# A gate's down-projection made transposed and turned by copies, with six output row buffers

## The chip, the cores and the metric

The kernel runs on one core of one Trainium2 chip. Its engines are TensorE (PE, with its weight loads shown as PEld), VectorE (DVE), ScalarE (ACT), GpSimd (POOL) and SyncE (SP), which issues nearly all copies. The metric is the device time of one execution in microseconds (us), the median of several runs.

## The reference

One attention layer and one gated feed-forward layer read the same normalised rows (2048 tokens, 640 features, all bf16). The feed-forward result, through a silu, gates the attention's result:

```python
xn = _layernorm(x, axis=-1)                       # x: 1 x 2048 x 640
# attention: 32 heads of 20, softmax over all 2048 keys
qkv = (xn @ wqkv).reshape(B, S, 3, 32, 20)
s = concat_heads(softmax(q @ k.T * 20**-0.5) @ v) @ wo
# gated feed-forward, 640 -> 1728 -> 640
h = sigmoid(xn @ w_gate) * (xn @ w_up)
g = silu(h @ w_down)
return x + s * g
```

(`concat_heads` stands for the transpose and reshape that put the 32 heads side by side again.)

## The kernel before

A first stage, about the first 30 us, loads the rows, normalises them and keeps them transposed in `xnT` (128 features on the partitions, 5 blocks of features, 4 chunks of 512 tokens). After it the kernel is one long stage whose instruction order on PE, ACT, DVE and POOL is written out by a planner: a loop over a modelled time `now` that picks, for each engine that is free in its model, the next piece of work. The chip then runs this order as it stands, engine by engine, with waits between the engines.

What the planner orders:

* Attention, in 32 blocks of 4 heads and 512 queries. PE makes score tiles (128 keys x 512 queries, line 900) into PSUM: two double banks `scA` that ACT reads with one exponential over 1024 columns (`pt`), and three single banks `bk`. A score tile in a single bank is either read by ACT (`px`, 512 columns) or by DVE, which makes the exponential itself in integer arithmetic (`iv`, then three passes over four tiles, `pb`). PE multiplies all of them with the values into `oacc` (line 937). At the end of a block `norm_a` and `norm_b` copy `oacc` (`on`), turn the sums of the exponentials by copies through DRAM (`ld`, `lt`), take a reciprocal on DVE (`rt`), spread it by copies (`rd`, `rl`), multiply on POOL (`on_bf`) and copy the result into `oU`.
* The feed-forward layer, `glu_items`, chunk by chunk: 14 gate and up projections (`mk_gu`) fill `hT` (hidden features on the partitions, 512 tokens), then the down-projection (`mk_down`). These items take one of the three single banks that the scores use too.
* The output projection (`mk_out`), two halves of 320 features for each of the first 12 token tiles: PE multiplies `oU` with `wo`, DVE multiplies the result with the gate row (`otmp`), POOL or DVE adds the row of x, and SP writes the result. The last chunk's four token tiles are made by a chain of their own at the very end (`chain`).

In the down-projection of before, an item is one token tile of 128 and one half of 320 features. `cols` puts each of its 14 steps on PE as four matmuls side by side that each use 32 columns of the array; the tokens' hidden values are the stationary operand and `wd` streams, 320 columns. ACT takes a tanh of the result (`td`), and DVE combines both (`gqs`, line 741; in the last chunk `gql`, line 737) to four times the silu. The result has tokens on the partitions, as the output needs it, in f32. For chunks 0 to 2 SP writes it to `gq_dram`; `load_out` later reads a token tile's row of it beside the row of x, into one of three buffers cut from `xnT`, for the token tile at hand and the one after it within a chunk. For the last chunk it stays in SBUF (`gq_last`).

What sets the order around the change: `LEAD` (how far, in us of PE work, the feed-forward items may run ahead of a due line), `M_ORD`, `DORD` and `XORD` (which of the three single banks an item, a DVE score tile or an extra ACT score tile takes first), the events `ev_at` that an item's `pre` waits for, and the list `timed`, whose entries are put into the SP queue when the model's time comes. SP issues its copies strictly in order, and a copy that waits holds those behind it. `timed` is one way for copies to get there; the others are issued with the instruction that makes their data.

Of the kernel before, what the change touches and what calls it, by code (L numbers as in the profile page):

```python
# [29 lines left out]

URGENT, ROUNDS, HOLD, SLACK, LEAD, LAG, D_LAST, D_LAST_END = 0.2, 6, 0.0, 0.0, 40.0, 2.0, 20, 20
M_ORD, WAIT3, FALL, M_END = 1, 0.2, 1, 2.0
NPT, NPX, NPB, NIV = 12, 5, 3, 3
DVE_ADD = 8
XMAX, DQ, DORD, XORD, STARVE = 2, 1.4, 2, 0, 0.3

# [16 lines left out]
def kernel(  # L53
# [40 lines left out]

    gq_dram = dram.tile([S, D], FP32, name="gq_dram", tag="gqd", bufs=1)
    NU = (HEADS - PG * GH) // UH
# [350 lines left out]
    T_IV, T_ON = 0.605, 0.60  # L447
    LATE, T_LT, T_OU, T_L2, T_RL = 1.0, 9.0, 1.5, 4.5, 5.6
    T_PASS = (0.1333, 0.1333, 0.27)
# [215 lines left out]
    def mk_gu(c, kf, at):  # L665
# [20 lines left out]
        def th():  # L686
            st["t"] = w2.tile([P, QC], BF16, tag="tnh", bufs=2, name="tnh")
            act_imm(st["t"][0:fs, :], st["g"][0:fs, :], ACT.Tanh, 0.5)
# [8 lines left out]
        def th2():  # L697
            st["t"] = w2.tile([P, QC], BF16, tag="tnh", bufs=2, name="tnh")
            act_imm(st["t"][fs:P, :], st["g"][0:fs, :], ACT.Tanh, 0.5)
# [13 lines left out]

    def gq_last(t4):
        if len(gq_l) == t4 // 2:
            w = w2.tile([P, 2, KD, 2 * P], BF16, tag="wgu", bufs=2, name="gql")
            gq_l.append(w.rearrange("p i k f -> p (i k f)").bitcast(FP32))
        return gq_l[t4 // 2][:, t4 % 2 * D:(t4 % 2 + 1) * D]

    def mk_down(c, t4, h, at):  # L720
        st = {}
        tt = 4 * c + t4

        def alloc():
            st["ps"] = misc_ps()

        def mm(kf):
            cols(st["ps"][:, 0:HD], hT[:, kf, t4 * P:(t4 + 1) * P], wd[:, kf, h * HD:(h + 1) * HD],
                 kf == 0, kf == NFT - 1)

        def th():
            st["td"] = w2.tile([P, HD], BF16, tag="td", bufs=2, name="td")
            act_imm(st["td"], st["ps"][:, 0:HD], ACT.Tanh, 0.25)

        def ev():
            if c == NQC - 1:
                return nc.vector.scalar_tensor_tensor(out=gq_last(t4)[:, h * HD:(h + 1) * HD], in0=st["td"], scalar=1.0,
                                                      in1=st["ps"][:, 0:HD], op0=ALU.add, op1=ALU.mult)
            flush("o")
            gqs = w2.tile([P, HD], FP32, tag="gqs", bufs=3, name="gqs")  # L740
            ins = nc.vector.scalar_tensor_tensor(out=gqs, in0=st["td"], scalar=1.0, in1=st["ps"][:, 0:HD],
                                                 op0=ALU.add, op1=ALU.mult)
# [13 lines left out]
    def div_scale(tps, n):  # L756
# [6 lines left out]
        return onq  # L763

    def load_out(tt):
# [4 lines left out]
        out_tiles[tt] = (o2[:, 0:D], o2[:, D:3 * D].bitcast(FP32))  # L770
        nc.sync.dma_start(out=out_tiles[tt][0], in_=x2[tt * P:(tt + 1) * P, :])
        nc.sync.dma_start(out=out_tiles[tt][1], in_=gq_dram[tt * P:(tt + 1) * P, :])

    def mk_out(tt, h, at):
        st = {}

        def alloc():
            if h == 0:
                load_out(tt)
                if (tt + 1) % 4:  # L780
                    load_out(tt + 1)
            st["ps"] = misc_ps()
# [5 lines left out]
        def ev():  # L788
            xr, gqr = out_tiles[tt]
            sl = slice(h * HD, (h + 1) * HD)  # L790
            while sum(x[1] == "o" for x in pool_q) > 2:
                x = next(x for x in pool_q if x[1] == "o")
                pool_q.remove(x)
                x[2]()
            tmp = w2.tile([P, 2 * HD], BF16, tag="gqs", bufs=3, name="otmp")[:, 0:HD]
            ins = nc.vector.scalar_tensor_tensor(out=tmp, in0=st["ps"][:, 0:HD], scalar=0.25,
                                                 in1=gqr[:, sl], op0=ALU.mult, op1=ALU.mult)

            if tt >= DVE_ADD:
                st["tmp"] = tmp  # L800
                return ins

            def part(i):
                cs = slice(h * HD + i * HD // 2, h * HD + (i + 1) * HD // 2)
                add = nc.gpsimd.tensor_tensor(out=xr[:, cs], in0=tmp[:, i * HD // 2:(i + 1) * HD // 2], in1=xr[:, cs], op=ALU.add)
                if h == 1 and i == 1:
                    nc.sync.dma_start(out=out2[tt * P:(tt + 1) * P, :], in_=xr)
                return add
            for i in range(2):
                pool_q.append((now + 0.6, "o", lambda i=i: part(i)))  # L810
            return ins
        def add():
            xr = out_tiles[tt][0][:, h * HD:(h + 1) * HD]
            ins = nc.vector.tensor_tensor(out=xr, in0=st["tmp"], in1=xr, op=ALU.add)
            if h == 1:
# [3 lines left out]
                     ("DVE", 0.40, ev, "free", mark("o", tt, h))] + ([("DVE", 0.24, add)] if tt >= DVE_ADD else []), at, need=ALT + 1 + 2 * (tt // 4),  # L819
                    pre=[("d", tt // 4, t4, i) for t4 in range(4) for i in range(2)] + [("h", 2, kf) for kf in range(NFT)] + (  # L820
                        [("o", tt - 2, 1)] if h == 0 and tt > 1 else []))
# [284 lines left out]
    def t_main(t4):  # L1106
        nc.vector.scalar_tensor_tensor(out=tmps[t4], in0=mains[t4], scalar=0.25, in1=gq_last(t4)[:, 0:512],
                                       op0=ALU.mult, op1=ALU.mult)
        if t4 < 2:
            nc.gpsimd.tensor_tensor(out=tail[t4][:, 0:512], in0=tmps[t4], in1=tail[t4][:, 0:512], op=ALU.add)  # L1110

    def t_rest(i):
        nc.vector.scalar_tensor_tensor(out=tmp[:, 2 * i:2 * i + 2, :],
                                       in0=rest[i][:, 0:2 * EX].rearrange("p (t e) -> p t e", e=EX),
                                       scalar=0.25, in1=gq_l[i].rearrange("p (t u) -> p t u", u=D)[:, :, 512:D],
                                       op0=ALU.mult, op1=ALU.mult)
# [422 lines left out]
```

## Time and profile before

| what | value |
|---|---|
| median of 3 runs | 802.37 us (801.88 to 803.19) |
| profiled execution | 803.29 us |
| its span, first to last instruction | 801.6 us |
| granted TensorE clock | 0.999 of full speed |
| PE / DVE / ACT / POOL busy | 97% / 96% / 98% / 12% of the span |
| bytes moved by copies | 60.47 MB, mean 75 GB/s |
| copies in the chain that ended last | 1% of the span |

The page gives for each engine the time in which some instruction of it was running. Instructions overlap their neighbours at both ends, so the time that one of them costs a full engine is the distance from its start to the next one's start, and not its length. A group's row gives line, engine, operation, names and shapes, then the count, the busy time in us, the mean length in ns, and the idle time of the engine just before its members with what ended it. A row of the timeline gives start and length in us. The chain of work that ended last is followed back from the last instruction, at each step to what released it.

### The profile page before, as it was taken

The page shows a single profiled execution, that of the slowest core. Times are in us where ns is not written, and L with a number is a line of the kernel's source. Part 1 is how long each engine was busy: PE and PEld are TensorE (multiplying, and loading weights), DVE is VectorE, ACT ScalarE, POOL GpSimd, SP SyncE. Part 2 cuts the span into 40 slices and gives each one's busy share as a digit, 9 for nine tenths or more (in the row PEclk, how much of TensorE's full clock was granted, in tenths as well). Part 3 has the DMA queues.
Part 4 walks back from the last instruction along what each step waited for, and adds up shares of the span by engine and source line. Part 5 has one row for each costly group of instructions (what it writes and reads, how often), then busy time and mean ns, then how long its engine had stood idle before and what let it go on. Part 6 is the DMA issues. An engine that isn't in the chain of part 4 may idle for free.

```text
span 801.6 us, 25384 instructions
## 1 busy us (share of the span) xinstructions
PE 779.8 (97%) x10465; PEld 284.4 (35%) x10465; DVE 770.1 (96%) x1246; ACT 781.8 (98%) x992; POOL 96.4 (12%) x203
## 2 busy tenths in 40 slices
PE   8899999999999999999999999999999999999997
PEld 5523333333433323334332332333333233333332
DVE  7798999999999999989999999999999999999997
ACT  8799999999999999999999999999999999999994
POOL 7200000000000000000000000000000100502302
PEclk9999999999999999999999999999999999999999
DMA  5441212223122223222113232222311332331421
GB/s 162 132 131 49 69 40 73 66 67 81 47 62 67 73 72 100 53 60 65 53 46 89 58 87 73 73 81 62 98 36 61 91 89 53 102 107 23 141 70 55
DMA packets 91851, 60.47 MB, mean 75 GB/s; under 512 B 34891, under 2 KB 85627, under 8 KB 91735
## 3 DMA queue, kind: packets, MB, share of 16 engines
q1 hardware_dynamic: 91447, 58.52, 26.1%
q8 instruction: 82, 1.34, 0.7%
q14 instruction: 34, 0.28, 0.1%
q10 hardware_dynamic: 288, 0.33, 0.1%
HBM read 45.18 MB, written 11.09 MB: 70 GB/s over the span
## 4 chain that ended last, share of the span: by engine, by line
PE 45%; ACT 41%; DVE 7%; issue 5%; DMA 1%; SPq 0%; POOL 0%; DVEq 0%; ACTq 0%; POOLq 0%
ACT pt L83 33%; PE bk L474 18%; PE scA L900 14%; PE oacc L937 9%; ACT px L83 4%; DVE iv L1336 2%; ACT tnh L83 2%; DVE pb L1036 1%; ACT td L83 1%; PE bk L900 1%; DVE pb L1033 1%; PE tp L293 1%; DVE pb L1030 0%; DMA lt<-ld 0%; DMA ld<-on 0%
## 5 line engine op out<-in xcount | busy, mean ns | idle before, releaser
L83 ACT ACTIVATE pt<-scA 128x1024 bf16<-128x1024 f32 (+1 forms) x709 | 708.7, 1188 | 0.7 <-PE bk L900 0.3
L1336 DVE TENSOR_SCALAR iv<-bk 128x512 int16<-128x512 f32 x499 | 332.2, 683 | 12.1 <-PE bk L900 9.6
L900 PE MATMUL scA<-q,kT 32*128 32x512 bf16 x1412 | 275.8, 382 | 8.8 <-ACT pt L83 3.3
L900 PE MATMUL bk<-q,kT 32*128 32x512 bf16 x636 | 207.3, 383 | 0.2 <-DVE iv L1336 0.2
L900 PEld LDWEIGHTS <-kT 32*128 32x128 bf16 x2048 | 88.4, 91 | 262.4 <-issue 251.1
L937 PE MATMUL oacc<-pt,v 128*21 128x512 bf16 x1412 | 178.5, 381 | 0.7 <-ACT pt L83 0.7
L937 PE MATMUL oacc<-pb,v 128*21 128x512 bf16 x998 | 160.8, 382 | 0.0
L474 PE MATMUL bk<-xnT,wgu 128*32 128x512 bf16 x2160 | 157.3, 383 | 0.5 <-DVE iv L1336 0.2
L1036 DVE TENSOR_TENSOR pb<-iv,pb 128x2048 bf16<-128x2048 bf16 (+1 forms) x125 | 151.8, 1214 | 0.7
L990 POOL TENSOR_TENSOR on_bf<-on,rl 128x128 bf16<-128x128 f32 x116 | 54.3, 472 | 626.8 <-DVE iv L1336 189.1
L83 ACT ACTIVATE px<-bk 128x512 bf16<-128x512 f32 x137 | 102.1, 762 | 1.7 <-POOL hT L1178 1.6
L474 PE MATMUL bk<-wd,hT 128*32 128x320 bf16 x1792 | 87.0, 302 | 0.1
L1030 DVE TENSOR_SCALAR pb<-iv 128x2048 int16<-128x2048 int16 (+1 forms) x125 | 86.0, 688 | 0.4
L1033 DVE TENSOR_SCALAR pb<-iv 128x2048 int16<-128x2048 int16 (+1 forms) x125 | 85.9, 688 | 0.0
L937 PEld LDWEIGHTS <-v 128*21 128x21 bf16 x2547 | 53.6, 91 | 76.2 <-issue 53.6
L474 PEld LDWEIGHTS <-wgu 128*32 128x32 bf16 x2160 | 44.5, 95 | 64.3 <-issue 46.3
L474 PEld LDWEIGHTS <-hT 128*32 128x32 bf16 x1792 | 37.5, 95 | 38.2 <-issue 32.7
L474 PE MATMUL bk<-xnT,wu 128*32 128x512 bf16 x640 | 48.5, 383 | 0.6 <-DVE iv L1336 0.2
L937 PE MATMUL oacc<-px,v 128*21 128x512 bf16 x137 | 47.0, 381 | 0.0
L83 ACT ACTIVATE tnh<-bk 128x512 bf16<-128x512 f32 (+1 forms) x56 | 43.4, 776 | 0.1
L691 DVE SCALAR_TENSOR_TENSOR hT<-tnh,bk 128x512 bf16<-128x512 bf16 x52 | 35.4, 680 | 1.0 <-PE bk L900 0.3
L655 PE MATMUL bk<-wv,xnT 128*128 128x160 bf16 x280 | 29.4, 235 | 0.6 <-ACT px L83 0.6
(120 smaller groups left out, 406.2 us busy)
## 6 DMA issues: line engine op xcount, KB each, us to landing
rl<-rd SPq DMA_DIRECT2D x124, 64.0 KB
wgu<-in_B_w_gate_dram SPq DMA_DIRECT2D x24, 320.0 KB
wgu<-in_B_w_up_dram SPq DMA_DIRECT2D x24, 320.0 KB
gq_dram<-gqs SPq DMA_DIRECT2D x24, 160.0 KB
xnT<-gq_dram SPq DMA_DIRECT2D x12, 320.0 KB
xt<-in_A_x_dram SPq DMA_DIRECT2D x16, 160.0 KB
xnT<-in_A_x_dram SPq DMA_DIRECT2D x16, 160.0 KB
out_dram<-xnT SPq DMA_DIRECT2D x14, 160.0 KB
```

Of the source, the lines that this page charges most:

```text
L83: return nc.scalar.add_instruction(mybir.InstActivation(func=func, name=nc.get_next_instruction_name(), engine=ENG.Activation, ins=[nc.sca ...
L293: nc.tensor.transpose(out=tps[k][:, kd, :], in_=xns[k][:, kd * P:(kd + 1) * P], identity=ident)
L474: nc.tensor.matmul(out[j:j + 32, :], lhsT=lhsT[:, j:j + 32], rhs=rhs, start=start, stop=stop, tile_position=(0, j), skip_group_check=True)
L655: nc.tensor.matmul(st["ps"][:, i * 2 * GC:(i + 1) * 2 * GC], lhsT=xn_tok(tts[i], kd), rhs=wvs[pr][:, kd, :], start=(kd == 0), stop=(kd == ...
L691: return nc.vector.scalar_tensor_tensor(out=hT[0:fs, kf, :], in0=st["t"][0:fs, :], scalar=1.0, in1=st["u"][0:fs, :], op0=ALU.add, op1=ALU. ...
L900: nc.tensor.matmul(dst, lhsT=kTs[gc_of(b)[0] % 2][32 * j:32 * j + 32, kt * P:(kt + 1) * P], rhs=qts[b % 3][32 * j:32 * j + 32, :], start=T ...
L937: nc.tensor.matmul(oacc[32 * j:32 * j + DH + 1, :], lhsT=lhsT, rhs=u["src"], start=first, stop=last, tile_position=(0, 32 * j), skip_group ...
L990: ins = nc.gpsimd.tensor_tensor(out=on_bf[:, cs], in0=on[:, cs], in1=rl[:, cs], op=ALU.mult)
L1030: ins = nc.vector.tensor_scalar(out=pb[:, 0, :, :].bitcast(I16), in0=iv, scalar1=0x7F80, scalar2=1, op0=ALU.bitwise_and, op1=ALU.bitwise_or)
L1033: ins = nc.vector.tensor_scalar(out=pb[:, 1, :, :].bitcast(I16), in0=iv, scalar1=0x007F, scalar2=0x3F00, op0=ALU.bitwise_and, op1=ALU.bitw ...
L1036: ins = nc.vector.tensor_tensor(out=pb[:, 1, :, :], in0=iv.bitcast(BF16), in1=pb[:, 1, :, :], op=ALU.mult)
L1336: beat(nc.vector.tensor_scalar(out=d["iv"][:, j, :], in0=bank[bk], scalar1=B_OFF, scalar2=0.0, op0=ALU.add, op1=ALU.max))
```

## The change

The down-projection of a chunk is made transposed. An item is now one tile of 128 output features (5 in a chunk) for all 512 tokens: `wd` is the stationary operand and `hT` streams, 512 columns. ACT's tanh and DVE's combination work on 128 features x 512 tokens, and the result is bf16. A transposing copy from SP turns it at once into four token tiles (`g4`, or straight into `gq_last` for the last chunk), and for chunks 0 to 2 a second copy writes `g4` to `gq_dram`, which is bf16 now. Both are entered in `timed`, 0.8 and 5.8 us of model time after the combination. `gqs` and `g4` have one buffer each; the tanh shares three buffers with that of the gate projection.

The output rows get six buffers of two bf16 rows (x and gate) instead of three, and each item's `alloc` may load one further row pair, up to four token tiles ahead, if its buffer is free and its chunk's gate is made. The planner's `LEAD` goes from 40 to 30, and the three bank orders change.

```diff
-URGENT, ROUNDS, HOLD, SLACK, LEAD, LAG, D_LAST, D_LAST_END = 0.2, 6, 0.0, 0.0, 40.0, 2.0, 20, 20
-M_ORD, WAIT3, FALL, M_END = 1, 0.2, 1, 2.0
+URGENT, ROUNDS, HOLD, SLACK, LEAD, LAG, D_LAST, D_LAST_END = 0.2, 6, 0.0, 0.0, 30.0, 2.0, 20, 20
+M_ORD, WAIT3, FALL, M_END = 0, 0.2, 1, 2.0
-XMAX, DQ, DORD, XORD, STARVE = 2, 1.4, 2, 0, 0.3
+AHEAD = 4
+XMAX, DQ, DORD, XORD, STARVE = 2, 1.4, 0, 1, 0.3
...
-    gq_dram = dram.tile([S, D], FP32, name="gq_dram", tag="gqd", bufs=1)
+    gq_dram = dram.tile([S, D], BF16, name="gq_dram", tag="gqd", bufs=1)
...
-    def mk_down(c, t4, h, at):
+    def mk_down(c, e, at):
...
         def mm(kf):
-            cols(st["ps"][:, 0:HD], hT[:, kf, t4 * P:(t4 + 1) * P], wd[:, kf, h * HD:(h + 1) * HD],
-                 kf == 0, kf == NFT - 1)
+            cols(st["ps"], wd[:, kf, e * P:(e + 1) * P], hT[:, kf, :], kf == 0, kf == NFT - 1)
 
         def th():
-            st["td"] = w2.tile([P, HD], BF16, tag="td", bufs=2, name="td")
-            act_imm(st["td"], st["ps"][:, 0:HD], ACT.Tanh, 0.25)
+            st["td"] = w2.tile([P, QC], BF16, tag="tnh", bufs=3, name="td")
+            act_imm(st["td"], st["ps"], ACT.Tanh, 0.25)
 
         def ev():
-            if c == NQC - 1:
-                return nc.vector.scalar_tensor_tensor(out=gq_last(t4)[:, h * HD:(h + 1) * HD], in0=st["td"], scalar=1.0,
-                                                      in1=st["ps"][:, 0:HD], op0=ALU.add, op1=ALU.mult)
-            flush("o")
-            gqs = w2.tile([P, HD], FP32, tag="gqs", bufs=3, name="gqs")
-            ins = nc.vector.scalar_tensor_tensor(out=gqs, in0=st["td"], scalar=1.0, in1=st["ps"][:, 0:HD],
+            gqs = w2.tile([P, QC], BF16, tag="gqs", bufs=1, name="gqs")
+            ins = nc.vector.scalar_tensor_tensor(out=gqs, in0=st["td"], scalar=1.0, in1=st["ps"],
                                                  op0=ALU.add, op1=ALU.mult)
-            nc.sync.dma_start(out=gq_dram[tt * P:(tt + 1) * P, h * HD:(h + 1) * HD], in_=gqs)
+            es = slice(e * P, (e + 1) * P)
+            g4 = w2.tile([P, 4, P], BF16, tag="g4", bufs=1, name="g4") if c < NQC - 1 else gq_last()[:, :, es]
+            timed.append((now + T_GT, lambda: nc.sync.dma_start_transpose(out=g4, in_=gqs)))
+            if c < NQC - 1:
+                timed.append((now + T_GO, lambda: nc.sync.dma_start(
+                    out=gq_dram[c * QC:(c + 1) * QC, es].rearrange("(t p) u -> p t u", p=P), in_=g4)))
             return ins
-        return Item([("PE", alloc, [(0.14, lambda kf=kf: mm(kf)) for kf in range(NFT)]),
-                     ("ACT", 0.32, th), ("DVE", 0.40, ev, "free", mark("d", c, t4, h))], at, pre=[("h", c, kf) for kf in range(NFT)])
+        return Item([("PE", alloc, [(T_MM, lambda kf=kf: mm(kf)) for kf in range(NFT)]),
+                     ("ACT", 0.48, th), ("DVE", 0.60, ev, "free", mark("d", c, e))], at, pre=[("h", c, kf) for kf in range(NFT)])
...
     def load_out(tt):
...
-        o2 = xfl[:, tt % 3 * KD * QC:tt % 3 * KD * QC + 3 * D]
+        o2 = xfl[:, tt % 6 * 2 * D:(tt % 6 + 1) * 2 * D]
...
         def alloc():
-            if h == 0:
-                load_out(tt)
-                if (tt + 1) % 4:
-                    load_out(tt + 1)
+            load_out(tt)
+            n = len(out_tiles)
+            if n < NOUT and n <= tt + AHEAD and (n < 6 or ("o", n - 6, 1) in ev_at) and all(
+                    ("d", n // 4, i) in ev_at for i in range(KD)):
+                load_out(n)
             st["ps"] = misc_ps()
...
-            tmp = w2.tile([P, 2 * HD], BF16, tag="gqs", bufs=3, name="otmp")[:, 0:HD]
+            tmp = w2.tile([P, HD], BF16, tag="ot", bufs=3, name="otmp")
...
-        for h in range(2):
-            for t4 in range(4):
-                glu.append(lambda at, c=c, t4=t4, h=h: [mk_down(c, t4, h, at)])
+        for e in range(KD):
+            glu.append(lambda at, c=c, e=e: [mk_down(c, e, at)])
```

More of the change, by code (lines that the diff above doesn't have):

```diff
@@ L447 @@
     T_IV, T_ON = 0.605, 0.60
-    LATE, T_LT, T_OU, T_L2, T_RL = 1.0, 9.0, 1.5, 4.5, 5.6
+    LATE, T_LT, T_OU, T_L2, T_RL, T_GT, T_GO = 1.0, 9.0, 1.5, 4.5, 5.6, 0.8, 5.8
     T_PASS = (0.1333, 0.1333, 0.27)
@@ L686, in th @@
         def th():
-            st["t"] = w2.tile([P, QC], BF16, tag="tnh", bufs=2, name="tnh")
+            st["t"] = w2.tile([P, QC], BF16, tag="tnh", bufs=3, name="tnh")
             act_imm(st["t"][0:fs, :], st["g"][0:fs, :], ACT.Tanh, 0.5)
@@ L697, in th2 @@
         def th2():
-            st["t"] = w2.tile([P, QC], BF16, tag="tnh", bufs=2, name="tnh")
+            st["t"] = w2.tile([P, QC], BF16, tag="tnh", bufs=3, name="tnh")
             act_imm(st["t"][fs:P, :], st["g"][0:fs, :], ACT.Tanh, 0.5)
@@ L712, with gq_last @@
     gq_l = []
-    def gq_last(t4):
-        if len(gq_l) == t4 // 2:
+    def gq_last():
+        if not gq_l:
             w = w2.tile([P, 2, KD, 2 * P], BF16, tag="wgu", bufs=2, name="gql")
-            gq_l.append(w.rearrange("p i k f -> p (i k f)").bitcast(FP32))
-        return gq_l[t4 // 2][:, t4 % 2 * D:(t4 % 2 + 1) * D]
-    def mk_down(c, t4, h, at):
+            gq_l.append(w.rearrange("p i k f -> p (i k f)")[:, 0:4 * D].rearrange("p (t u) -> p t u", u=D))
+        return gq_l[0]
+    def mk_down(c, e, at):
         st = {}
-        tt = 4 * c + t4
         def alloc():
@@ L763, in div_scale @@
         return onq
+    NOUT = 4 * (NQC - 1)
     def load_out(tt):
@@ L767, in load_out @@
             return
-        o2 = xfl[:, tt % 3 * KD * QC:tt % 3 * KD * QC + 3 * D]
+        o2 = xfl[:, tt % 6 * 2 * D:(tt % 6 + 1) * 2 * D]
         flush("o")
-        out_tiles[tt] = (o2[:, 0:D], o2[:, D:3 * D].bitcast(FP32))
+        out_tiles[tt] = (o2[:, 0:D], o2[:, D:2 * D])
         nc.sync.dma_start(out=out_tiles[tt][0], in_=x2[tt * P:(tt + 1) * P, :])
@@ L819, in mk_out @@
                      ("DVE", 0.40, ev, "free", mark("o", tt, h))] + ([("DVE", 0.24, add)] if tt >= DVE_ADD else []), at, need=ALT + 1 + 2 * (tt // 4),
-                    pre=[("d", tt // 4, t4, i) for t4 in range(4) for i in range(2)] + [("h", 2, kf) for kf in range(NFT)] + (
+                    pre=[("d", tt // 4, i) for i in range(KD)] + [("h", 2, kf) for kf in range(NFT)] + (
                         [("o", tt - 2, 1)] if h == 0 and tt > 1 else []))
@@ L1106, in t_main @@
     def t_main(t4):
-        nc.vector.scalar_tensor_tensor(out=tmps[t4], in0=mains[t4], scalar=0.25, in1=gq_last(t4)[:, 0:512],
+        nc.vector.scalar_tensor_tensor(out=tmps[t4], in0=mains[t4], scalar=0.25, in1=gq_last()[:, t4, 0:512],
                                        op0=ALU.mult, op1=ALU.mult)
@@ L1114, in t_rest @@
                                        in0=rest[i][:, 0:2 * EX].rearrange("p (t e) -> p t e", e=EX),
-                                       scalar=0.25, in1=gq_l[i].rearrange("p (t u) -> p t u", u=D)[:, :, 512:D],
+                                       scalar=0.25, in1=gq_last()[:, 2 * i:2 * i + 2, 512:D],
                                        op0=ALU.mult, op1=ALU.mult)
```

## The prediction

> **What bounds the kernel now.** I read the page's busy line first, then the chain that ended last, then the groups of instructions, and last the timeline, because two of the engines are full and only the distance from one start to the next says what an instruction costs there.
>
> ```profile
> span 801.6 us, 25384 instructions
> ## 1 busy us (share of the span) xinstructions
> PE 779.8 (97%) x10465; PEld 284.4 (35%) x10465; DVE 770.1 (96%) x1246; ACT 781.8 (98%) x992; POOL 96.4 (12%) x203
> ...
> PE 45%; ACT 41%; DVE 7%; issue 5%; DMA 1%; SPq 0%; POOL 0%; DVEq 0%; ACTq 0%; POOLq 0%
> ```
>
> Three engines are busy 96 to 98%, and the chain changes hands between PE (45%) and ACT (41%). No DMA holds it for more than 1%. The groups that the change touches, by form:
>
> ```profile
> L474 PE MATMUL bk<-wd,hT 128*32 128x320 bf16 x1792 | 87.0, 302 | 0.1
> L83 ACT ACTIVATE td<-bk 128x320 bf16<-128x320 f32 x32 | 19.8, 618 | 0.0
> L741 DVE SCALAR_TENSOR_TENSOR gqs<-td,bk 128x320 f32<-128x320 bf16 x24 | 11.6, 483 | 0.7 <-ACT td L83 0.7
> L796 DVE SCALAR_TENSOR_TENSOR otmp<-bk,xnT 128x320 bf16<-128x320 f32 x24 | 11.5, 481 | 0.0
> L737 DVE SCALAR_TENSOR_TENSOR gql<-td,bk 128x320 f32<-128x320 bf16 x8 | 3.8, 475 | 0.0
> ```
>
> Durations overlap their neighbours, so I price by spacing of starts. Timeline rows (start, length):
>
> ```profile
> 204.47 0.48 DVE L741 SCALAR_TENSOR_TENSOR gqs<-td,bk 128x320 f32<-128x320 bf16 x1
> 204.87 0.68 DVE L1336 TENSOR_SCALAR iv<-bk 128x512 int16<-128x512 f32 x1
> 205.47 0.68 DVE L1030 TENSOR_SCALAR pb<-iv 128x2048 int16<-128x2048 int16 x1
> ...
> 209.08 0.60 ACT L83 ACTIVATE td<-bk 128x320 bf16<-128x320 f32 x1
> 209.40 0.78 ACT L83 ACTIVATE px<-bk 128x512 bf16<-128x512 f32 x1
> 209.87 1.22 ACT L83 ACTIVATE pt<-scA 128x1024 bf16<-128x1024 f32 x1
> 210.78 0.81 ACT L83 ACTIVATE px<-bk 128x512 bf16<-128x512 f32 x1
> ...
> 215.24 0.86 PE L474 MATMUL bk<-wd,hT 128*32 128x320 bf16 x20
> ...
> 303.09 1.26 PE L474 MATMUL bk<-xnT,wgu 128*32 128x512 bf16 x20
> 304.28 0.39 PE L900 MATMUL scA<-q,kT 32*128 32x512 bf16 x2
> ```
>
> DVE pays 0.40 us for a 320-wide eviction and 0.60 for a 512-wide one; ACT pays 0.32 (td), 0.47 (512 wide) and 0.91 (1024 wide). Four column matmuls start together, so 20 of them are five groups: (0.86 - 0.30)/4 = 0.140 us a group at 320 columns, (1.26 - 0.38)/4 = 0.22 at 512. Five groups from 303.09 would let the next start at 304.19; it starts at 304.28, so a change between score matmuls and others costs about 0.1 us. ACT stands nearest to its floor: from 40 to 760 us the starts of its instructions are only some 13 us later in all than those spacings added up. So ACT's own work, and what PE does to hand it scores late, set the time.
>
> **The change part by part.** The down-projection now makes 20 items (4 chunks, 5 feature tiles) of 14 groups where there were 32 (4 token tiles, 2 halves, 4 chunks) of 14.
>
> PE: 448 groups x 0.140 = 62.7 us become 280 x 0.22 = 61.6: 1.1 us less. At strictly the same price per column (0.140 x 1.6 = 0.224) it would be nothing, so this term lies between 0 and 1.1. The fewer weight loads (1792 to 1120) count nothing: PEld is 35% busy and runs under the matmuls.
>
> ACT: 32 x 0.32 = 10.2 us become 20 x 0.47 = 9.4: 0.8 less. DVE: 32 x 0.40 = 12.8 become 20 x 0.60 = 12.0: 0.8 less. The gate in bf16 makes the out evictions no cheaper: 320 wide they take 481 ns reading an f32 gate and 475 to 483 with a bf16 tanh.
>
> The planner's settings (LEAD, and the order in which free banks are taken) re-deal the whole issue order. The built order shows what that does to the work: score tiles for DVE 499 before and after; exponentials 703 double, 6 halved and 137 single become 701, 7 and 140, which is -1.8 + 0.5 + 1.4 = +0.1 us for ACT; changes between score matmuls and others on PE fall from 1442 to 1424, 18 x 0.1 = 1.8 us less. How tightly the order fits cannot be read from counts; I take no change, and as bounds 3 us either way, about a quarter of ACT's 13 us.
>
> Copies: 24 writes of the gate (160 KB) go from the SP queue; 20 transposing copies and 15 writes (128 KB each) come in, 11 entries more. At 0.35 us of issue a piece (8.9 us for the 24) that is 4 us on a queue whose issues add up to some two fifths of the span; all of it lies beside the engines while nothing waits for a landing. What now waits: `gqs` and `g4` have one buffer each, so the next down eviction on DVE waits until the last transposition has landed, and the next transposition waits for the write that empties `g4`. Behind that eviction on DVE stand the score evictions and passes, and for the banks they free PE and then ACT wait. Behind a write that waits for its transposition on SP stand `lt`, `rd`, `rl` and the q loads; behind `lt` stands DVE's reciprocal, which in the trace waited 1.5 us in 2 of 31 cases. No transposition is in the trace. The nearest rows are copies of the chain of waits:
>
> ```profile
> 4.56 3.21 DMA wst<-in_A_wqkv_dram
> ...
> 728.06 1.53 DMA lt<-ld
> ```
>
> that is 1.5 us (8 KB) to 3.2 us (100 KB in short runs). I take 3.2, the nearer in size. Against it stands the cover: adding spacings between neighbouring `gqs` evictions in the built order, the shortest distance is 7.1 us (11 instructions), the others in a chunk 7.2 to 9.5 or more. Less 0.7 for the eviction and 0.4 for issue, some 6.0 us are free for landing. At 3.2 us nothing waits: cost 0; both ends of the row's range give 0 as well, and past 6 us it costs what rival B says. Ahead of the last blocks the `ld` copies stand behind transpositions too; there I allow 0 to 1.5 us, take 0.
>
> On the price of a transposition, the Trainium skill (VectorE: DVE Perf Modes, The three transpose paths) gives 1309 ns for a 128x128 one by DMA; an estimate for four in turn is 5.2 us, which would still cost 0. No run here shows it yet.
>
> Rows: x and gate rows loaded up to four token tiles ahead, in six buffers, 160 KB of gate instead of 320. The evictions that need them idled 0.0 us (L796 above), so the earlier loads bring 0; they take bytes from DMA engines busy about a quarter of the time.
>
> Sum: PE 1.1 + 1.8 = 2.9 us less, ACT 0.7, DVE 0.8. Not all of it lies on the path. Weighted with the chain's shares it is 0.45 x 2.9 + 0.41 x 0.7 + 0.07 x 0.8 = 1.3 + 0.3 + 0.1 = 1.7 us. The profiled execution took 803.3 us (span 801.6, 1.7 around it), so 801.6; the median of the runs is 0.9 lower, 802.37, so 800.7. I say 800.6. If only ACT's work counted, the gain is 0.7 (801.7); if the savings of all three added up, 4.4 (798.0); with 3 us either way for the order, 796 to 804.
>
> **The rivals.**
> A. A wash. ACT is at its floor, so PE's saving turns into PE idling: 802.37 - 0.7 = 801.7. For it: ACT starts are only 13 us late over 720. Against: PE holds more of the chain than ACT. Small terms of either sign also end here.
> B. Slower through the single `gqs` buffer. If a transposition lands L us after its issue, an eviction that follows after d waits L + 1.1 - d. It decides from L = 6. At L = 8, with distances 7.1, 7.1, 7.2, 8.3, 8.3, 8.3, 8.4, seven waits of 2.0, 2.0, 1.9, 0.8, 0.8, 0.8 and 0.7 make 9 us; DVE has little slack (96%), so most reaches the end: 800.6 + 7 = 808. For it: nothing in the trace bounds a transposition, and SP's order can delay its issue behind q loads that wait for PE (34.5 us in 29 cases). Against: every landing in the chain is under 3.3 us. Beside it: the Trainium skill (Advanced Engine Details and Errata, DGE: Hardware vs Software) rates transposes issued from the hardware queues worse than others; its next section calls them as fast as regular copies. No run here shows which.
> C. The new order fits worse: with 30 instead of 40 us of lead and other banks, ACT's 13 us grow to 18: 805 to 806. For it: the order is static, so each late bank costs ACT at once. Against: fewer changes of family on PE.
> D. The rows ahead do nothing, since nothing waited for them. That is already in the sum.
>
> **How the numbers follow.** Forecast with its kin (a gain of 1.6 us or more) 0.42; A 0.27; B 0.14; C 0.17. The likeliest time is 800.6, its own range 797.5 to 801.6. About 0.2%, 1.6 us, is what a measurement can tell from no change: below 800.8 is faster, so the forecast lies close to that border, and A is the neighbour on the other side. The whole range runs from 797.0 (the full savings and a little of the order) to 807.5 (most of B): some 0.1 each side is left out. Faster 0.42, same 0.27, slower 0.31 (B and C).
>
> **What would show it.** Right: 1120 down matmuls about 0.22 apart in fives, `td` 512 wide x20 spaced 0.47, `gqs` x20 spaced 0.60 with idle below 1 us and not ended by a DMA, ACT busy about 1 us less, chain still PE and ACT. B would show as `gqs` waiting for a DMA on DVE and long transposition waits in SP's own waits; C as longer gaps before `pt` and `iv` with PE named. Wrong altogether: a chain with SP or DMA of several per cent, or a difference above 8 us.

## The result, and the profile after

The changed kernel takes 804.33 us (median, 803.24 to 805.10), the kernel before 802.71 us beside it on the same chip (801.88 to 803.58). The ratio is 1.0020, with an interval of 1.0014 to 1.0027: slower by 1.6 us. The forecast was a gain of about 1.8 us. The profiled execution of the changed kernel took 803.43 us, low among its runs, so its span of 801.7 us must not be set against the 801.6 of before: what the page shows is where the time lies, and the size of the loss comes from the medians.

The page of the changed kernel, its span, busy times and the first line of the chain that ended last:

```profile
span 801.7 us, 24011 instructions
## 1 busy us (share of the span) xinstructions
PE 772.7 (96%) x9788; PEld 262.5 (33%) x9793; DVE 768.6 (96%) x1234; ACT 781.4 (97%) x982; POOL 99.7 (12%) x203
...
ACT 56%; PE 20%; DVE 12%; issue 9%; POOL 1%; DMA 0%; SPq 0%; DVEq 0%; ACTq 0%; POOLq 0%
```

PE is busy 7.1 us less than before, DVE 1.5, ACT 0.4, and nothing of it shows in the time. The chain that PE held for 45% has gone over to ACT (41 to 56%). The groups of the down-projection, by form:

```profile
L475 PE MATMUL bk<-hT,wd 128*32 128x512 bf16 x1120 | 82.6, 383 | 2.7 <-DVE iv L1338 2.3 <-DVE hT L703 0.2
L84 ACT ACTIVATE td<-bk 128x512 bf16<-128x512 f32 x20 | 14.5, 726 | 0.0
L736 DVE SCALAR_TENSOR_TENSOR gqs<-td,bk 128x512 bf16<-128x512 bf16 x20 | 13.6, 682 | 0.8 <-ACT td L84 0.6
L799 DVE SCALAR_TENSOR_TENSOR otmp<-bk,xnT 128x320 bf16<-128x320 f32 x24 | 11.6, 483 | 0.3 <-PE bk L475 0.2
```

`gqs` idles 0.8 us over 20 evictions, and no copy is named for any of its waits, so its single buffer costs nothing. The one new large wait is DVE's reciprocal `rt` waiting for the denominators `lt`. The waits of DVE, first after, then before (line, waited for, us in total, times, longest):

```profile
DVE rt L982 <- DMA lt<-ld: 2.9, 2, 2.7
```

```profile
DVE rt L980 <- DMA lt<-ld: 1.5, 2, 0.8
```

Nearly all of it stands in block 28 (of 0 to 31). The timeline of the changed kernel there shows how it is handed on:

```profile
731.92 0.25 DVE L982 RECIPROCAL rt<-lt 128x16 f32<-128x16 f32 x1 [2.65 <-DMA lt<-ld]
...
734.63 1.26 PE L475 MATMUL bk<-hT,wd 128*32 128x512 bf16 x20 [2.15 <-DVE iv L1338]
...
736.32 1.94 ACT L84 ACTIVATE pt<-scA 128x1024 bf16<-128x1024 f32 x2 [1.96 <-PE bk L902]
```

DVE stands still for 2.65 us; the score eviction behind the reciprocal frees its bank late, PE idles 2.15 us ahead of 20 down-projection matmuls, and the scores queued behind these reach ACT 1.96 us late. In the kernel before the same reciprocal waited 0.79 us:

```profile
729.62 0.25 DVE L980 RECIPROCAL rt<-lt 128x16 f32<-128x16 f32 x1 [0.79 <-DMA lt<-ld]
```

The SP queue at that place, first of the changed kernel, then of the kernel before (start, length of the issue):

```profile
725.08 0.76 SPq L1022 DMA_DIRECT2D oU<-on_bf  x1
725.95 1.23 SPq L740 DMA_TRANSPOSE gql<-gqs  x1
727.24 0.75 SPq L1022 DMA_DIRECT2D oU<-on_bf  x1
728.09 0.53 SPq L974 DMA_DIRECT2D ld<-on  x1
728.67 1.50 SPq L1022 DMA_DIRECT2D oU<-on_bf  x2
730.28 0.42 SPq L976 DMA_DIRECT2D lt<-ld  x1
```

```profile
723.98 2.27 SPq L1020 DMA_DIRECT2D oU<-on_bf  x3
726.36 0.53 SPq L972 DMA_DIRECT2D ld<-on  x1
726.93 0.73 SPq L1020 DMA_DIRECT2D oU<-on_bf  x1
728.06 0.35 SPq L974 DMA_DIRECT2D lt<-ld  x1
```

The copy `on`, from which `ld` reads, stands at nearly the same time in both (723.73 and 723.38). From `lt`'s issue to `rt` it is 1.6 us in both. What differs lies ahead of `lt`: the queue's head, an `oU` copy that waits for GpSimd's product `on_bf`, starts 1.1 us later (GpSimd makes the block's four products from 723.35 us on; before, it had made the first at 720.68 and began the other three at 722.48), and a transposition is issued among the rest, 1.23 us long. Together 2.3 us, which is the distance of the two reciprocals (731.92 and 729.62).

### The profile page after: what moved, and what is told of

It reads as the page before. It is cut to its first block, busy times and chain, and to the rows that moved or that the text cites. A ratio compares the mean times of both kernels' runs of the same rounds, so it can differ in the third digit from the quotient of the medians.

```text
span 801.7 us, 24011 instructions
## 1 busy us (share of the span) xinstructions
PE 772.7 (96%) x9788; PEld 262.5 (33%) x9793; DVE 768.6 (96%) x1234; ACT 781.4 (97%) x982; POOL 99.7 (12%) x203
## 4 chain that ended last, share of the span: by engine, by line
ACT 56%; PE 20%; DVE 12%; issue 9%; POOL 1%; DMA 0%; SPq 0%; DVEq 0%; ACTq 0%; POOLq 0%
ACT pt L84 44%; PE bk L475 8%; ACT px L84 6%; PE scA L902 6%; DVE iv L1338 5%; PE oacc L939 4%; ACT tnh L84 3%; DVE pb L1038 2%; DVE pb L1032 1%; DVE pb L1035 1%; ACT td L84 1%; DVE hT L692 1%; PE psk L144 0%; PE bk L656 0%; ACT aq L175 0%
## 5 line engine op out<-in xcount | busy, mean ns | idle before, releaser
L84 ACT ACTIVATE pt<-scA 128x1024 bf16<-128x1024 f32 x708 | 698.1, 1162 | 2.3 <-PE bk L902 2.0
L902 PE MATMUL bk<-q,kT 32*128 32x512 bf16 x639 | 202.9, 384 | 0.2
L939 PE MATMUL oacc<-pt,v 128*21 128x512 bf16 x1409 | 185.1, 382 | 1.0 <-ACT pt L84 1.0
L902 PEld LDWEIGHTS <-kT 32*128 32x128 bf16 x2048 | 85.3, 91 | 288.0 <-issue 278.3
L475 PE MATMUL bk<-xnT,wgu 128*32 128x512 bf16 x2160 | 159.1, 383 | 0.8
L84 ACT ACTIVATE px<-bk 128x512 bf16<-128x512 f32 x140 | 100.3, 729 | 2.0 <-POOL hT L1180 1.6
L475 PE MATMUL bk<-hT,wd 128*32 128x512 bf16 x1120 | 82.6, 383 | 2.7 <-DVE iv L1338 2.3
L84 ACT ACTIVATE tnh<-bk 128x512 bf16<-128x512 f32 (+1 forms) x56 | 41.3, 738 | 0.1
L475 PEld LDWEIGHTS <-wd 128*32 128x32 bf16 x1120 | 20.7, 95 | 35.6 <-issue 29.2
```

Of the source, the lines that this page charges most:

```text
L84: return nc.scalar.add_instruction(mybir.InstActivation(func=func, name=nc.get_next_instruction_name(), engine=ENG.Activation, ins=[nc.sca ...
L475: nc.tensor.matmul(out[j:j + 32, :], lhsT=lhsT[:, j:j + 32], rhs=rhs, start=start, stop=stop, tile_position=(0, j), skip_group_check=True)
L902: nc.tensor.matmul(dst, lhsT=kTs[gc_of(b)[0] % 2][32 * j:32 * j + 32, kt * P:(kt + 1) * P], rhs=qts[b % 3][32 * j:32 * j + 32, :], start=T ...
L939: nc.tensor.matmul(oacc[32 * j:32 * j + DH + 1, :], lhsT=lhsT, rhs=u["src"], start=first, stop=last, tile_position=(0, 32 * j), skip_group ...
```

## The experiments

Names of the theories: T, the loss is this wait of `rt` for `lt` in the tail; A, as in the prediction, ACT at its floor so that PE's savings turn into idling; S, the planner's settings. In the later runs P stands for PE's work counting by its share of the chain (in e12: PE and DVE holding the time as much as ACT), O for the new order as a whole (in e11: entries on SP are hidden), Q for the place of the copies on the SP queue. Each ratio is to the kernel before on the same chip, whose medians there were 802.75 to 803.05. The changed kernel was not run again beside them: where a run is set against its 804.33 us, some 0.3 us can come from the occasion alone, since the kernel before took 802.71 us then.

**e1. The kernel before once more** (no edit).

> The kernel before, unchanged, as a control. All theories: ratio 1.000, interval within 0.999 to 1.001. What it tells apart is the granted clock of its single runs. If the changed kernel's extra 1.6 us came from TensorE being slowed near 30 us (its granted clock was 0.994 in 7 of 16 runs, 0.998 in 6), this one would show 0.998 throughout; if both kernels show the same mixture of clocks, the clock is no part of the difference.

Measured 802.81 us, ratio 1.0001 (0.9993 to 1.0010). So differences of 0.1% can be told apart in these runs. Of the clocks it shows a mixture, but not that of the changed kernel: 0.994 in 2 of 11 runs here and in 6 of the 120 runs of the kernel before beside all the experiments, against 7 of 16 runs of the changed kernel. Those 7 took 804.83 us in the median, the other 9 803.96, so the clock seems to have a part in the loss; the last section comes back to it.

**e2. All transpositions of the last chunk later.** They are tied to a later DVE instruction, and `gqs` alternates between two buffers there:

```diff
...
-            timed.append((now + T_GT, lambda: nc.sync.dma_start_transpose(out=g4, in_=gqs)))
+            def turn():
+                x = nc.sync.dma_start_transpose(out=g4, in_=gqs)
+                if c == NQC - 1:
+                    tc.add_manual_dep(x.ins, dve_ins[0].ins.name, SYNC, reason="turned behind lt")
+            timed.append((now + (T_GT if c < NQC - 1 else 7.0), turn))
```

> The changed kernel; only in the last chunk the transposing copies are issued later, behind the lt copy (and gqs takes g4's buffer in turn there, so that nothing waits for them). The order on PE, ACT and DVE is the same. Theory T (the tail: 1.23 us of SP issue of a transposition stands ahead of ld and lt near 727 us, rt waits 2.65 us there instead of 0.79): the wait of rt falls to about 1.4 us and the time by 1.2 us, from 804.3 to 803.1, ratio to before about 1.0005. Theory S (the planner's new settings fit worse): time unchanged, 804.3, ratio 1.002. Theory B of the prediction (gqs buffer): unchanged as well, no gqs wait to remove.

Measured 806.21 us, ratio 1.0035 (1.0022 to 1.0048): T expected it under the changed kernel; it is 1.9 us above in the median (the intervals overlap a little). The wait in block 28 fell to 1.68 us, near the 1.4 expected, but another transposition now came to stand just ahead of `lt` in block 29:

```profile
751.62 1.23 SPq L741 DMA_TRANSPOSE gql<-gqs  x1
752.94 0.52 SPq L980 DMA_DIRECT2D lt<-ld  x1
```

and the reciprocal behind it, at 756.3, waited 2.21 us. The wait had been moved, not removed.

**e3. The transpositions as plain copies** of the same tile (the turn is left out, so the gate's rows are in the wrong places).

```diff
-            timed.append((now + T_GT, lambda: nc.sync.dma_start_transpose(out=g4, in_=gqs)))
+            timed.append((now + T_GT, lambda: nc.sync.dma_start(out=g4, in_=gqs.rearrange("p (t u) -> p t u", u=P))))
```

> The changed kernel with all 20 transposing copies as plain copies of the same bytes between the same tiles (the turn itself is left out). Theory T: SP issues each in about 0.4 us instead of 1.23, so ld near 728 us is issued 0.85 us earlier: time 0.8 to 0.9 us less than the changed kernel, 803.5, ratio 1.001. Theory S: 804.3, ratio 1.002. If landings of transpositions held something up elsewhere, the gain would be more than 1.5 us.

Measured 803.78 us, ratio 1.0011 (1.0003 to 1.0020): 0.55 us under the changed kernel's median, less than the 0.8 to 0.9 expected, and with intervals that overlap, so the time alone settles nothing here. The same place on the queue:

```profile
726.43 0.67 SPq L740 DMA_DIRECT2D gql<-gqs  x1
```

The entry takes 0.67 us of issue where the transposition takes 1.23, and the reciprocal's wait falls by 0.53 us (2.65 to 2.12). At this place the entry costs DVE about what it takes to issue.

**e4. The settings alone, in the kernel before.**

```diff
-URGENT, ROUNDS, HOLD, SLACK, LEAD, LAG, D_LAST, D_LAST_END = 0.2, 6, 0.0, 0.0, 40.0, 2.0, 20, 20
-M_ORD, WAIT3, FALL, M_END = 1, 0.2, 1, 2.0
+URGENT, ROUNDS, HOLD, SLACK, LEAD, LAG, D_LAST, D_LAST_END = 0.2, 6, 0.0, 0.0, 30.0, 2.0, 20, 20
+M_ORD, WAIT3, FALL, M_END = 0, 0.2, 1, 2.0
...
-XMAX, DQ, DORD, XORD, STARVE = 2, 1.4, 2, 0, 0.3
+XMAX, DQ, DORD, XORD, STARVE = 2, 1.4, 0, 1, 0.3
```

> The kernel before with only the four planner settings changed (LEAD 30, M_ORD 0, DORD 0, XORD 1). Theory S (the re-dealt order costs the 1.6 us): 804 to 805, ratio 1.002 or more. Theory T: the settings are about neutral, 802 to 803.5, ratio 0.999 to 1.001, unless the new order moves the tail's ld copies, which its trace would show as a changed wait of rt for lt.

Measured 811.47 us, ratio 1.0112 (1.0095 to 1.0129), more than either theory expected. The wait of DVE that grew most is again that of `rt` for `lt`, from 1.5 to 6.1 us, the longest of it in block 29:

```profile
DVE rt L980 <- DMA lt<-ld: 6.1, 4, 3.7
```

**e5. The changed kernel without that wait.** Block 27 keeps its denominators (`lt0`), and the last reciprocals read those, so all waits of `rt` for `lt` are gone (2.9 us in all, 2.65 of them in block 28). The computation is wrong by it; the copies are still made:

```diff
...
-        beat(nc.vector.reciprocal(out=rt, in_=lt), False)
+        beat(nc.vector.reciprocal(out=rt, in_=lt if b < NBLK - 4 else lt0[0]), False)
```

> The changed kernel with every instruction in its place, but the reciprocals of the last four blocks read the denominators of an earlier block, which landed long before (so the attention of four blocks is divided by the wrong numbers). The copies ld and lt are still made. T (the loss is the wait for lt at 731.9 us, 2.65 us, handed on to PE and ACT): 2 to 3 us below the changed kernel, 801.7, ratio to the kernel before 0.998 to 0.999. O (the new order as a whole fits worse, the wait at 731.9 only stands where the time is lost anyway): 804.3, ratio 1.002. T also expects the 3.3 us gap of ACT at 736 to close to about 1.

Measured 801.59 us, ratio 0.9983 (0.9975 to 0.9992): 2.7 us less than the changed kernel, as T expected.

**e6. The same edit in the kernel before.**

> The same edit in the kernel before (attention of four blocks divided by the wrong numbers), whose rt waited 1.5 us in two places, 0.8 the longest. T: 0.5 to 1.0 us below the kernel before, ratio 0.999, and within 0.7 us of the changed kernel with the same edit: without this wait the two kernels are the same. O: no change, 802.7, and the changed kernel stays 1.5 us above.

Measured 802.33 us, ratio 0.9991 (0.9982 to 0.9999). Without these waits the changed kernel is faster than the kernel before by 0.7 us (802.33 against 801.59, on the same chip; 11 runs each, 801.87 to 802.91 against 801.09 to 802.11); with them, it is slower by 1.6. The sign of the whole change hangs on these waits.

**e7. Half of the down-projection's matmuls left out** (so the gate is half a sum). In effect:

```diff
-            cols(st["ps"], wd[:, kf, e * P:(e + 1) * P], hT[:, kf, :], kf == 0, kf == NFT - 1)
+            if kf % 2 == 0:
+                cols(st["ps"], wd[:, kf, e * P:(e + 1) * P], hT[:, kf, :], kf == 0, kf == NFT - 2)
```

> The changed kernel with every second group of the down-projection's matmuls left out (7 of 14 a tile; the gate is then half a sum), the order of all else as it was. PE has 20 x 7 x 0.22 = 31 us less to do. A (ACT stands at its floor, PE's savings turn into idling): 0 to 3 us less than the changed kernel, 801.5 to 804.3, PE's busy time 742, ACT's unchanged. P (PE's time counts by its share of the chain, 0.20 after, 0.45 before): 6 to 14 us less, 790 to 798.

Measured 805.32 us, ratio 1.0031 (1.0020 to 1.0043). PE has 140 groups of matmuls less, some 31 us by their spacing, and the kernel gains nothing: P falls, and A comes nearest, though not even its 0 to 3 us less came. (PE's busy time came to 757.9 us and not to the 742 expected; where the rest went was not followed up.) The tail can't have hidden a gain: the copy `on` of block 28, ahead of which 504 of the 560 matmuls left out would have stood, comes at 724.1 us, against 723.7 in the changed kernel, though PE was busy 16.4 us less up to 724 us (689.4 against 705.7). The median is 1.0 us above the changed kernel's, with intervals that overlap; in the tail the windows show PE's clock at half speed after the same stall (columns: window and its length in us, busy us of PE, PEld, DVE, ACT, POOL with their instructions, then the granted clock, the copies' share and their GB/s):

```profile
732.00:736.00 4.00, 1.59 (x23) 0.59 (x15) 3.65 (x6) 2.76 (x4) 0.00 (x0) 0.74 0.13 36
736.00:740.00 4.00, 4.00 (x33) 0.66 (x25) 3.05 (x6) 2.31 (x3) 0.00 (x0) 0.50 0.31 64
740.00:744.00 4.00, 4.00 (x36) 0.90 (x33) 3.52 (x5) 3.30 (x4) 0.46 (x1) 0.50 0.02 4
```

**e8. The changed kernel with the settings of before** (the diff above, turned round).

> The changed kernel with the planner's settings of the kernel before (LEAD 40, M_ORD 1, DORD 2, XORD 0). The kernel before lost 8.7 us by the new settings, mostly in waits of rt for lt in its last 100 us. S (the settings fit one structure, each order has its own luck in the tail): slower than the changed kernel by 1 to 8 us, 805 to 812, with rt waiting for lt longer than 2.9 us in all. If the old settings were simply better: 800.5 to 803, faster than the changed kernel.

Measured 804.27 us, ratio 1.0018 (1.0009 to 1.0027): the same as the changed kernel. Its `rt` waits 2.2 us, at another block. Both expectations missed: the settings that cost the old structure 8.6 us (e4) are worth nothing either way in the new one.

**e9 and e10. The reciprocal planned later** (`T_L2` 7.0 instead of 4.5, in both kernels).

> The changed kernel with the planned distance from the copy `on` to the reciprocal of the last blocks raised (T_L2 7.0 instead of 4.5), so that the reciprocals of blocks 28 to 30 stand some 2.5 us later on DVE; the computation is whole. T (the loss is the wait for lt in block 28, where on to rt took 8.19 us against 5.46 when nothing is waited for): the wait of 2.65 us falls under 0.5, 801.6 to 802.6, ratio 0.998 to 1.000. O (the new order fits worse as a whole): 804.3. Against T: what is normalised later may make the out-projection of the last chunk late, up to 2.5 us, 804.

Measured 804.19 us, ratio 1.0015 (1.0006 to 1.0023). The wait in block 28 fell to 0.36 us as expected (one of 0.81 came in block 29), and the time did not follow. The setting deals the issue order of the whole tail anew, and the new order has its own hole, PE waiting for ACT's `pt` twice for 1.0 us (at 759.4 and 764.3 us), with the clock at half behind it:

```profile
756.00:764.00 8.00, 5.36 (x52) 1.48 (x50) 7.93 (x12) 7.75 (x10) 1.78 (x1) 1.00 0.25 53
764.00:768.00 4.00, 3.20 (x28) 0.84 (x31) 3.83 (x7) 3.62 (x6) 0.00 (x0) 0.57 0.08 21
768.00:771.00 3.00, 3.00 (x35) 0.88 (x27) 2.55 (x5) 2.44 (x3) 0.00 (x0) 0.50 0.00 0
```

> The same setting in the kernel before, whose rt waited 0.79 and 0.66 us. T: at most the 0.7 us that the kernel gained when these waits were taken away, so 802.0 to 802.8, ratio 0.999 to 1.000, and the changed kernel with the same setting 0.2 to 1.0 us under it. If a later rt makes the end late, 803 to 805.

Measured 802.64 us, ratio 0.9999 (0.9990 to 1.0007): nothing, and the changed kernel with this setting is 1.6 us above it, not under it as expected. Taken alone these two runs can't tell T from a worse order, since they change both.

**e11. More entries on SP in the kernel before**, all other engines' orders as they were. In effect, just ahead of `ld`:

```diff
+        for _ in range(2 * (b == NBLK - 4)):
+            nc.sync.dma_start(out=dram.tile([GH, QC], FP32, name="lx", tag="lx"), in_=on.rearrange("(j r) q -> j r q", r=32)[:, 0, :])
```

> The kernel before with every instruction in its place on PE, ACT and DVE, and two more copies of the denominators beside ld of block 28, 0.53 us of issue each on the SP queue (to rows that nothing reads). T (a queue entry ahead of lt costs what it takes to issue, on DVE's reciprocal, and the time follows): rt of block 28 waits 0.79 + 1.06 = 1.85 us instead of 0.79, the time rises by 0.6 to 1.1, 803.6 to 804.1. O: entries on SP are hidden, 803.0 as the kernel before in these runs.

Measured 804.62 us, ratio 1.0028 (1.0019 to 1.0036). The two entries take 1.09 us, and the reciprocal's wait grows by 1.2 us:

```profile
725.74 1.09 SPq L971 DMA_DIRECT2D lx<-on  x2
...
730.21 0.25 DVE L980 RECIPROCAL rt<-lt 128x16 f32<-128x16 f32 x1 [1.99 <-DMA lt<-ld]
```

The time rose by 1.8 us, more than the wait itself and more than the 0.6 to 1.1 expected (4 of its 11 runs had a mean clock of 0.993 or 0.994). So two more entries at this place, 1.1 us of issue, make the kernel before as slow as the changed kernel, with no other order touched.

**e12. Less work for ACT in the changed kernel.**

```diff
-            act_imm(st["td"], st["ps"], ACT.Tanh, 0.25)
+            act_imm(st["td"], st["ps"][:, 0:P], ACT.Tanh, 0.25)
...
-            ins = nc.vector.scalar_tensor_tensor(out=gqs, in0=st["td"], scalar=1.0, in1=st["ps"],
+            ins = nc.vector.scalar_tensor_tensor(out=gqs, in0=hT[:, 0, :], scalar=1.0, in1=st["ps"],
```

> The changed kernel with the 20 tanh of the down-projection over 128 of their 512 columns, and the gate's evictions reading hT in their place, so DVE's and PE's work is the same (the gate is wrong). By the slope of the 320 and 512 wide rows one takes 0.17 instead of 0.47 us on ACT: 6.0 us less there. A (ACT is the engine that sets the time): 4 to 6 us less than the changed kernel, 798.3 to 800.3. P (PE and DVE hold it as much): 0 to 2 us less, 802.3 to 804.3.

Measured 801.64 us, ratio 0.9979 (0.9970 to 0.9988), 2.7 us less than the changed kernel: between the two expectations.

```profile
PE 772.5 (97%) x9793; PEld 261.7 (33%) x9793; DVE 768.1 (96%) x1234; ACT 776.8 (97%) x982; POOL 98.6 (12%) x203
...
ACT 44%; PE 31%; DVE 15%; issue 7%; SPq 1%; DMA 1%; POOL 0%; DVEq 0%; ACTq 0%; POOLq 0%
```

One tanh now takes 0.16 us from its start to the next, 0.32 less, and block 28's `on` comes 3.4 us earlier (720.3 instead of 723.7). By then 18 of the 20 are done, 5.8 us less for ACT, so before the tail some six tenths of what ACT saves arrive; of PE's saving in e7 nothing does. (The evictions no longer wait for the tanh either, 0.6 us in all in the changed kernel.) In the tail the wait in block 28 is 2.88 us here, and the clock stood at half for 3.4 us behind it; that these take the rest is likely and was not tried.

**f1. One transposition behind the reciprocal.** The computation is whole, and the orders of PE, ACT, DVE and POOL are those of the changed kernel. (`gqs` alternates between two buffers in the last chunk.)

```diff
-            timed.append((now + T_GT, lambda: nc.sync.dma_start_transpose(out=g4, in_=gqs)))
+            turn = lambda: nc.sync.dma_start_transpose(out=g4, in_=gqs)
+            after_rt.append(turn) if (c, e) == (NQC - 1, 2) else timed.append((now + T_GT, turn))
...
+        for f in after_rt if b == NBLK - 4 else ():      # in norm_b, behind the rl copies
+            tc.add_manual_dep(f().ins, dve_ins[0].ins.name, SYNC, reason="behind the reciprocal")
```

> The changed kernel, the computation whole and every instruction of PE, ACT, DVE and POOL in its place; on the SP queue one transposition alone (the third feature tile of the last chunk) is issued behind the reciprocal of block 28 instead of ahead of its ld. Q (the wait of rt is the sum of what stands ahead of lt on the queue: 1.23 us for this transposition, the rest for oU copies that GpSimd holds until 725.05): the wait falls from 2.65 to about 1.4 us, 803.0 to 803.8. O (order): 804.3.

Measured 802.57 us, ratio 0.9996 (0.9987 to 1.0005); the wait is 1.62 us, 1.03 less. The reciprocal:

```profile
731.23 0.25 DVE L985 RECIPROCAL rt<-lt 128x16 f32<-128x16 f32 x1 [1.62 <-DMA lt<-ld]
```

One transposition of the twenty, moved by some 6 us (from 725.95 to 731.91), takes back the 1.6 us that the change had lost, more than the wait itself and more than expected.

**f2. The `oU` copies of block 27 behind the reciprocal**, the transposition where it was (`after_rt` is issued as in f1):

```diff
-            if b < NBLK - 3:
+            if b == NBLK - 5:
+                after_rt.append(lambda o=o, x=x: nc.sync.dma_start(out=o, in_=x))
+            elif b < NBLK - 3:
```

> The changed kernel, the computation whole, PE, ACT, DVE and POOL in place; the four oU copies of block 27 (which nothing needs before the end) are issued behind the reciprocal of block 28 instead of ahead of its ld and lt; the transposition stays. Q: SP reaches ld at 725.1 instead of 728.1, lt lands some 3 us earlier, the wait of 2.65 us is gone, and the time is that of the kernel without this wait, 801.4 to 802.2, ratio 0.998 to 0.999. O: 804.3.

Measured 802.15 us, ratio 0.9989 (0.9981 to 0.9998): faster than the kernel before. Its SP queue, and the reciprocal:

```profile
724.18 1.21 SPq L740 DMA_TRANSPOSE gql<-gqs  x1
725.49 0.52 SPq L974 DMA_DIRECT2D ld<-on  x1
728.45 0.36 SPq L976 DMA_DIRECT2D lt<-ld  x1
```

```profile
730.03 0.25 DVE L982 RECIPROCAL rt<-lt 128x16 f32<-128x16 f32 x1 [0.42 <-DMA lt<-ld]
```

**f3. Both moves.**

> Both moves, the computation whole. Q: the same as the move of the oU copies alone, 801.4 to 802.2, since the wait can't fall below nothing. If transpositions cost in another way than by their place on SP, it would lie between this and 804.3.

Measured 802.13 us, ratio 0.9990 (0.9981 to 0.9999); the wait in block 28 is gone, 0.76 us are left in block 30. The same as the `oU` move alone, as expected. Its `ld` and `lt`:

```profile
724.25 0.50 SPq L977 DMA_DIRECT2D ld<-on  x1
725.93 0.36 SPq L979 DMA_DIRECT2D lt<-ld  x1
```

**f4. The `oU` move in the kernel before.**

> The kernel before with the four oU copies of block 27 moved the same way, the computation whole. Q: its wait of 0.79 us in block 28 goes, that of 0.66 in block 29 stays: 0.2 to 0.6 us less than the kernel before, 802.2 to 802.6, and the changed kernel with the same move some 0.7 us faster than this.

Measured 802.44 us, ratio 0.9996 (0.9987 to 1.0005): not to be told from the kernel before. The changed kernel with both moves is 0.3 us under it (802.13 against 802.44) and not the 0.7 expected; the intervals of the two ratios overlap.

## Why the prediction was wrong

**The step that failed is the last sentence on the copies**: "Ahead of the last blocks the `ld` copies stand behind transpositions too; there I allow 0 to 1.5 us, take 0". The value was not nothing, and it lay beyond the 1.5 allowed: the wait of `rt` for `lt` in block 28 grew by 1.86 us, from 0.79 to 2.65, and without this kind of wait (e5) the kernel takes 2.7 us less. Two errors are in it. The issue of an entry, transpositions with the rest, was sized at 0.35 us, the length of the copies they replace; a transposition takes 1.23, so twenty are some 25 us of issue, where 4 were counted for all the entries more. And 0 was chosen because the queue lies beside the engines while nothing waits for it, though the trace of before said that this place was not so: `rt` waited there already, so there was no cover left, and each further entry cost about its whole issue (e3, e11). f1 shows the part of the transposition (1.03 of 1.86 us of added wait). The rest goes with the later `on_bf` on GpSimd, part of the new order, which f2 goes round; why `on_bf` came later was not tried.

**PE's 2.9 us, weighted by 0.45, failed too**, and with it 1.3 of the 1.7 us of forecast gain. The spacing was right (20 matmuls in 1.26 us), the saving arrived as busy time, 7.1 us less in fact, and nothing shows that any of it arrived in the time. The chain's share of an engine was read as its price. It tells through whom the last chain ran, with three engines nearly full. e7 shows that in the changed kernel less work on PE had no price at all; the kernel before, where PE had 45%, was not tried so.

**ACT's 0.7 us fits**, and with it rival A's mechanism: where the waits are taken out of both kernels, the difference is 0.74 us (e5 and e6), beside A's 0.7, and e7 and e12 say that ACT's work counts and PE's does not. That the 0.74 is ACT's saving and nothing else is not shown (ACT's busy time fell by 0.4 us, DVE's by 1.5), so part of the agreement may be luck. Rival A was the body of the kernel, and the tail put 2 us on top of it. With each run set against the kernel before on its own chip, e5 is 1.5 us under it, e6 0.7 under and the changed kernel 1.6 over: the waits cost the new kernel 3.1 us and the old one 0.7, and without them the change is worth 0.7. These figures add up to the 1.6 by the way they are made; the sum is no further evidence.

**The landing of the transpositions came out as forecast** (cost 0, rival B wrong): no `gqs` waited for one. How long one takes to land is not in the rows. On the Trainium skill's (Advanced Engine Details and Errata, X-Bar Transpose (TRN2)) sentence that transposes by DMA are as fast as regular ones: no run here tells their transfers apart, but the issue on SP took 1.23 us against 0.67 for a plain copy of the same tile, and that is what counted.

**"I take no change" for the planner's settings** held for the new structure (e8) and would have been off by 8.6 us for the old (e4). Rival C's size (805 to 806) was near by luck, its place was not: added up from 80 to 720 us, ACT's starts come about 12 us later than the shortest usual spacing of each kind of instruction allows, in both kernels alike. The rows loaded ahead were not tried alone; `otmp` idled 0.0 us before and 0.3 after, in line with the 0 they were given.

## What to carry to other kernels

Before an entry is added to an in-order queue, look for the consumer on that queue that already waits, however little: there about the entry's whole issue time counts, and a full engine behind it hands it on to the others. The share of an engine in the chain is no price; with several engines nearly full, ask which of them has no slack, by taking work away from one at a time. And a setting that deals a static order anew is no clean test of a cause; moving a single copy, with all engines' orders kept, was.

## What the runs showed of the hardware that was not expected

* A transposing copy of a 128x512 bf16 tile between places in SBUF holds the SP queue 1.24 us (median of 20 in the changed kernel, 1.20 to 2.50), a plain copy of the same tile 0.54 (median of 20 in e3, 0.47 to 1.82).
* A copy issued right behind a transposition lands late: `ld` behind one took 2.96 us from its issue to that of `lt`, which waits for it (f2, 725.49 to 728.45), against 1.68 without one ahead (f3, 724.25 to 725.93); in e2 `lt` behind one took 3.4 us to the reciprocal against 1.6. Why was not tried.
* PE stalls of 1 to 3 us can halve its clock. After the stalls in the tail the granted clock stood at 0.5 for 3.4 us (e4, e12), 6.8 (e2, e9) and 10.2 (e7), in steps of 3.41 us. The Trainium skill (TensorE: Matmul & The Clock Gate, Part 1: The HAM clock gate) tells of a window of 3413 ns and of an idle one ahead of the slower clock; the step agrees, but the windows ahead of these spells had PE busy for 0.14 to 0.71 of their length, and others at 0.61 and 0.62 were followed by the full clock, so the point where it decides stays open. One spell of 3.4 us at half speed lowers the mean clock by 0.002 and costs at most 1.7 us (an estimate, half its length). 14 of the 18 traces have one such spell in their first 34 us, so a run at 0.994 has likely one more. The changed kernel had 0.994 in 7 of 16 runs, e5 and f1 to f3, in which its wait is shorter or gone, in 2 of 44. So the slower clock is rare where this wait is short, and may be why f1 gained more than the wait itself became shorter; that the spells of those 7 runs lie behind this stall is likely, and not shown: the changed kernel's own trace has none there.
